# DeltaNet followed by soft mixture of experts on one core: last token group routed in two halves, three experts' second weights loaded into buffers that attention has finished with, outputs stored two tokens a row

## The chip, the cores and the metric

The kernel runs on one core of one Trainium2 chip. The metric is device time in microseconds (us) of one execution. The time before is 323.27 us, the median of three runs (322.57 to 325.41 us). The profile is of a fourth execution that took 327.15 us; from its first to its last instruction it spans 325.4 us, and all times inside the profile are counted from the start of that span.

## The reference: what is computed

First a DeltaNet recurrence over 768 tokens, for 4 batches and 8 heads of size 48, in float32:

```python
k_n = k / (np.linalg.norm(k, axis=-1, keepdims=True) + 1e-06)
for t in range(S):
    y[:, :, t] = q_t @ state
    v_old = state^T @ k_t
    state = state + beta_t * outer(k_t, v_t - v_old)
```

The output y becomes x with 3072 rows (batch times token) and 384 columns. Then a soft mixture of 8 experts with 4 slots each (32 slots):

```python
logits = x @ phi                                   # 3072 x 32
d = softmax of logits over the 3072 tokens         # one maximum per slot, over all tokens
slot_input = d.T @ x                               # 32 x 384
h = relu(slot_input[e] @ w1[e]); slot_out[e] = h @ w2[e]     # w1: 384 x 1024, w2: 1024 x 384
c = softmax of logits over the 32 slots
out = c @ slot_out                                 # 3072 x 384
```

w1 and w2 are 12.6 MB each; one expert's w2 is 1.57 MB (1536 KB in the profile's list of DMA issues). The output is 4.7 MB.

## The kernel before, in words

**Attention.** The 768 tokens are cut into 24 chunks of 32, and the loop variable x runs over the chunks. Six groups n of four chunks (c = 0 to 3) share one 32 x 32 triangular inverse per head and batch, which DVE computes (`invert`, lines 265 to 408) one group ahead. In groups 0 to 4, DVE works on the next group's inverse; in the last group (x = 20 to 23) it has none to do. Inside chunk x the carried chain is: PE multiplies the old state with keys (L450 into psR) and queries (L450 into psY); DVE forms R (L457); PE solves with the inverse Tb (L464); ACT copies the result to U (L467); PE updates the state in PSUM (L477, not in the last chunk) and ACT copies it to S (L484); PE adds the within-chunk part of the outputs (L494) and ACT copies them to Y (L497). At the end of chunk x, `weights(x+1)` has ACT make the next Tb (L427, two instructions).

**Routing.** `turn` (L508) transposes a finished chunk's Y one chunk later. `route` (L516) handles one group: logits (L524), the largest logit per slot and row (L532), its transposition (L537), the maximum over the four batches (L545), its spreading over the partitions by eight small matmuls (L571), the running maximum (L579), the exponentials for the sum over tokens (L587), their repetition and masking (L597, L606), and the sum itself (L615, 32 matmul records for two chunks). Beside it run the softmax over slots (L541, L552 to L564). These pieces are hung into the chunks of the following group at hooks: "head" before R, "act" before the solve, "mid" after the solve and `turn`, "vec" just before the update, "end" after the outputs and before `weights(x+1)`. `late` is what is left for the first chunk of the group after that. Up to the end of the loop and the two drains behind it, each engine runs its instructions in the order in which they are written (`manual_schedule`, L674 to L828).

**The tail.** The last group is routed as a whole after the loop (L829 to L831), in an order that a scheduler chooses. Then the pools of attention are closed (L832), PSUM is handed to a new pool, and the experts run: `first(q)` for experts 4q to 4q+3 is two products (L890) with a mask and relu (L894, L897) and eight transposes (L903); `second(q)` is L914, accumulating into pso. Then pso is copied (L937), summed over batches and spread by one matmul (L939), scaled (L941), and multiplied with the transposed softmax cT for 24 tiles of 128 tokens (L947). Each tile is copied from PSUM by ACT or DVE (L951, L953) into one of ten buffers and stored by a DMA of 128 rows of 1536 bytes (L954).

**Queues.** Nearly all DMAs are issued by SP, in the order written: keys, queries and values some chunks ahead, then w1 into buffers of attention that are done (`preload`, with the table `free`, L755), then w2. A DMA that has to wait for its buffer holds up all those behind it on SP. Of w2, experts 0 to 4 go into new buffers (L841) laid over the space of the closed pools, experts 5 to 7 into the buffers of w1 of experts 0 to 3 (L926 to L931), which become free when `first(0)` has read them.

Of the kernel before, what the change touches and what calls it, by code (L numbers as in the profile page):

```python
# [17 lines left out]
def kernel(  # L18
# [49 lines left out]
    ps = att.enter_context(tc.tile_pool(name="ps", bufs=1, space=PSUM))  # L68
    io = att.enter_context(tc.tile_pool(name="io", bufs=2))
    wk = att.enter_context(tc.tile_pool(name="wk", bufs=2))  # L70
    psp = att.enter_context(tc.tile_pool(name="psp", bufs=1, space=PSUM))
# [7 lines left out]
    Ks = [io.tile([P, U, DP], F32, name=f"K{i}", bufs=1) for i in range(NK)]  # L79
# [20 lines left out]
    def load_v(cc, eng=nc.sync):  # L100
        Vt[cc] = io.tile([P, U, D], F32, name="V", tag="V", bufs=5)
        load(v, Vt[cc], cc, eng)
# [6 lines left out]
    one = cpool.tile([P, 1], F32, name="one")  # L109
    nc.vector.memset(one, 1.0)  # L110
    low = cpool.tile([P, 1], F32, name="low")
    nc.vector.memset(low, -15.0 * math.log(2.0))
    St = [wk.tile([P, 4, B, GD], F32, name=f"S{i}", bufs=1) for i in range(2)]
# [23 lines left out]
    nc.vector.tensor_reduce(own, hm.rearrange("p (y x) -> p x y", x=2), axis=AX.X, op=ALU.add)  # L137

# [54 lines left out]
    cells = [(e, k) for e in range(1, E) for k in range(NKT)]  # L193

# [12 lines left out]
    def preload(tags):  # L207
        for tag in tags.split():
            t = room(tag)
            for i in range(2 if tag == "GQ" else 1):  # L210
                e, k = cells.pop(0)
                load_w1(e, [k], t[:, i * F:(i + 1) * F])

# [294 lines left out]
    def turn(c, Yn, yT):  # L508

        py = pt([GD, B, P])  # L510
        for b in range(B):
            nc.tensor.transpose(py[:, b, :], Yn[:, c, b, 0:GD], ident)  # L512
        nc.scalar.activation(yT[:, :, :, c, :], py.rearrange("p b (h t) -> p b h t", h=4),
                             ACT.Copy)

    def route(n, Yn, yT):  # L516
        st = {}

        def logits():

            pl = st["pl"] = pt([P, P])
            for h in range(4):
                for b in range(B):
                    nc.tensor.matmul(pl[C * b:C * b + C], lhsT=phi[:, h, :],  # L524
                                     rhs=yT[:, b, h].rearrange("p c t -> p (c t)"),
                                     start=(h == 0), stop=(h == 3), skip_group_check=True)
            lT = st["lT"] = wk.tile([P, P], F32, name="lT", tag="lT", bufs=1)
            nc.scalar.activation(lT, pl, ACT.Copy)

        def maxima():  # L530
            m1 = st["m1"] = small.tile([P, 1], F32, name="m1", tag="m1")
            nc.vector.tensor_reduce(m1, st["lT"], axis=AX.X, op=ALU.max)  # L532

        def over_rows():

            pm = st["pm"] = pt([1, B, NSL])
            nc.tensor.transpose(pm.rearrange("p b s -> p (b s)"), st["m1"], ident)  # L537

        def by_tokens():
            pq = st["pq"] = pt([P, B, NSL])  # L540
            nc.tensor.transpose(pq.rearrange("p b s -> p (b s)"), st["lT"], ident)  # L541

        def rows_max():
            mr = st["mr"] = small.tile([1, NSL], F32, name="mr", tag="mr")
            nc.vector.tensor_reduce(mr, st["pm"].rearrange("p b s -> p s b"), axis=AX.X,  # L545
                                    op=ALU.max)

        def over_slots():
# [3 lines left out]
            nc.vector.tensor_reduce(mx, st["pq"], axis=AX.X, op=ALU.max)  # L552
            nc.vector.tensor_tensor(el, st["pq"], mx.unsqueeze(2).broadcast_to([P, B, NSL]),
                                    op=ALU.subtract)

        def slots_exp():
            nc.scalar.activation(st["el"], st["el"], ACT.Exp)

        def shares():
            sm, el = small.tile([P, B], F32, name="sm", tag="sm"), st["el"]  # L560
            nc.vector.tensor_reduce(sm, el, axis=AX.X, op=ALU.add)
            nc.vector.tensor_scalar(sm, sm, 1e-9, None, op0=ALU.add)
            nc.vector.reciprocal(sm, sm)
            nc.vector.tensor_tensor(Call[:, n], el, sm.unsqueeze(2).broadcast_to([P, B, NSL]),  # L564
                                    op=ALU.mult)

        def spread_max():

            pb = st["pb"] = pt([P, 1])
            for b in range(B):  # L570
                nc.tensor.matmul(pb[C * b:C * b + C], lhsT=st["mr"], rhs=one[0:1],  # L571
                                 start=True, stop=True, skip_group_check=True)

        def run_max():
            new, old = nrun[n % 2], nrun[1 - n % 2]
            if n == 0:
                nc.vector.tensor_scalar(new, st["pb"], -1.0, None, op0=ALU.mult)
            else:
                nc.vector.scalar_tensor_tensor(new, st["pb"], -1.0, old, op0=ALU.mult,  # L579
                                               op1=ALU.min)  # L580
                al = st["al"] = small.tile([P, 1], F32, name="al", tag="al")
                nc.vector.tensor_tensor(al, new, old, op=ALU.subtract)

        def rows_exp():
# [3 lines left out]
                dT, st["lT"].rearrange("p (c t) -> p c t", t=C).unsqueeze(2).broadcast_to(  # L588
                    [P, GC, 4, C]), ACT.Exp, bias=nrun[n % 2])
            if n:  # L590
                nc.scalar.activation(st["al"], st["al"], ACT.Exp)

        def repeat():

            pd = st["pd"] = pt([P, GC, B, NSL])
            for c in range(GC):
                nc.tensor.matmul(  # L597
                    pd[:, c].rearrange("p b s -> p (b s)"),
# [3 lines left out]
        def heads():  # L602

            dr = st["dr"] = wk.tile([P, GC * B, 2, NSL], F32, name="dr", tag="dr", bufs=1)
            for x in range(2):
                nc.scalar.activation(dr[:, :, x, :], st["pd"].rearrange("p c b s -> p (c b) s"),  # L606
                                     ACT.Identity, scale=own[:, x:x + 1])

        def slots(cs):
            pa = st["pa"] = pt([P, GD + 1])  # L610
            for c in cs:
                for b in range(B):
                    for y in range(2):
# [4 lines left out]
                            stop=(c == cs[1] and b == B - 1), skip_group_check=True)  # L618
# [364 lines left out]
```

## Time and profile before

| what | value |
|---|---|
| median of three runs | 323.27 us |
| profiled execution | 327.15 us, span 325.4 us |
| PE busy | 269.7 us (83%) |
| DVE busy | 219.7 us (68%) |
| ACT busy | 163.9 us (50%) |
| POOL busy | 160.5 us (49%) |
| mean granted TensorE clock | 0.897 |
| moved by DMA | 45.23 MB, 39.47 MB of it read |
| last attention product (L494) ends | 257.5 us |
| first expert product (L890) starts | 276.0 us |
| last product of second(1) (L914) ends | 305.9 us |
| first output DMA (L954) is issued | 309.6 us |

Busy shares are over the whole span. The last four rows divide the tail into stages that follow each other; what a change in a stage is worth has to be read from that stage. In the views, "pt", "psR", "psS", "psY" are PSUM tiles of attention; "tr", "ph", "po", "pso" those of the experts; "w2t", "wGQ", "wKQ", "w" are buffers of weights. "SPq" is SP's DMA queue; a "wait" there is SP standing still before it may issue.

### The profile page before, as it was taken

The numbers are of one execution on the slowest core, as the hardware profiler recorded it, in microseconds if no ns is written. First come the engines' busy times: TensorE is split into PE (matmuls) and PEld (weight loads), VectorE is DVE, ScalarE is ACT, GpSimd is POOL, SyncE is SP. The second block draws the span as 40 slices with busy tenths as digits, with TensorE's granted clock in tenths as the row PEclk, the third lists the DMA queues.
The fourth block names the chain that finished last, engine by engine and source line by source line (L and its number), as shares of the span: only waits on it lengthen the run. The fifth ranks groups of instructions, "written<-read, shape, count | busy, mean of one in ns | idle before, by whom it ended". The sixth has DMA issues, their size and how long they took to land.

```text
span 325.4 us, 16112 instructions
## 1 busy us (share of the span) xinstructions
PE 269.7 (83%) x6887; PEld 217.0 (67%) x6887; DVE 219.7 (68%) x798; ACT 163.9 (50%) x341; POOL 160.5 (49%) x342
## 2 busy tenths in 40 slices
PE   2896747888979999799998998796999958996890
PEld 2774546767868888688886887786888746332350
DVE  8289989987699989679799999998122122020161
ACT  2454236765857875367666865464358531120050
POOL 8949086784858299621999069996220000000000
PEclk9958559999999999679999999787899977999995
DMA  8955455455444456455201567437622653998087
GB/s 132 164 100 90 69 91 94 70 88 89 81 79 82 78 83 129 93 82 130 50 13 26 144 175 220 91 87 259 202 69 66 221 218 112 432 422 341 4 308 273
DMA packets 82503, 45.23 MB, mean 139 GB/s; under 512 B 74240, under 2 KB 77472, under 8 KB 81664
## 3 DMA queue, kind: packets, MB, share of 16 engines
q1 hardware_dynamic: 80640, 42.98, 50.5%
q0 software_dynamic: 704, 1.03, 1.7%
q8 instruction: 54, 0.88, 1.2%
q10 hardware_dynamic: 1088, 0.20, 0.3%
q14 instruction: 17, 0.14, 0.1%
HBM read 39.47 MB, written 4.72 MB: 136 GB/s over the span
## 4 chain that ended last, share of the span: by engine, by line
PE 50%; DVE 27%; DMA 8%; ACT 6%; issue 4%; SPq 3%; DVEq 0%; ACTq 0%
PE psR L464 6%; PE pt L615 6%; PE psS L477 6%; DMA wGQ<-in_moe_w_dram 5%; DVE prM L333 5%; PE psY L494 5%; PE psR L450 4%; PE pt L257 4%; PE pt L228 4%; DVE prE L333 4%; DVE nm L338 4%; PE pt L512 3%; DVE tt L338 3%; ACT S L484 2%; PE psY L450 2%
## 5 line engine op out<-in xcount | busy, mean ns | idle before, releaser
L414 POOL TENSOR_SCALAR V<-V,nT 128x48 f32<-128x48 f32 x192 | 90.4, 494 | 19.4 <-DMA V<-in_v_dram 5.7
L422 POOL TENSOR_SCALAR_AFFINE_SELECT Ab<-GQ 32x256 f32<-32x256 f32 x96 | 48.0, 500 | 16.9 <-PE psY L494 12.7
L484 ACT ACTIVATE S<-psS 48x768 f32<-48x768 f32 x46 | 37.0, 805 | 24.5 <-PE psS L477 24.2
L464 PE MATMUL psR<-R,Tb 64*64 64x48 f32 x768 | 29.0, 224 | 9.4 <-DVE R L457 6.4
L257 PE MATMUL pt<-KQ 48*32 48x64 f32 (+1 forms) x1792 | 25.9, 232 | 12.5 <-ACT KQ L244 8.8
L464 PEld LDWEIGHTS psR<-R,Tb 64*64 64x64 f32 x768 | 26.0, 139 | 13.0 <-issue 7.0
L257 PEld LDWEIGHTS pt<-KQ 48*32 48x32 f32 x1792 | 20.8, 116 | 18.7 <-ACT KQ L244 10.6
L333 DVE TENSOR_TENSOR prM<-tt,lb 128x16 f32<-128x16 f32 (+7 forms) x96 | 30.4, 317 | 0.0
L338 DVE TENSOR_TENSOR nm<-nm,prM 128x16 f32<-128x16 f32 (+7 forms) x96 | 30.2, 314 | 0.0
L494 PE MATMUL psY<-U,Ab 64*64 64x48 f32 x768 | 29.7, 231 | 0.1
L494 PEld LDWEIGHTS psY<-U,Ab 64*64 64x64 f32 x768 | 26.6, 145 | 2.7 <-issue 0.8
L261 ACT ACTIVATE GQ<-pt 128x256 f32<-128x256 f32 (+1 forms) x56 | 16.7, 351 | 21.4 <-PE pt L257 21.1
L467 ACT ACTIVATE U<-psR 128x384 f32<-128x384 f32 x24 | 11.8, 490 | 29.6 <-PE psR L464 28.3
L477 PE MATMUL psS<-U,K 32*112 32x96 f32 x736 | 26.4, 285 | 0.0
L457 DVE TENSOR_TENSOR R<-V,psR 128x384 f32<-128x384 f32 x24 | 13.2, 551 | 19.4 <-PE psR L450 13.1
L427 ACT ACTIVATE Tb<-TT,own 128x256 f32<-128x256 f32 x48 | 21.6, 504 | 8.1 <-DVE TT L405 8.1
L477 PEld LDWEIGHTS psS<-U,K 32*112 32x112 f32 x736 | 22.4, 189 | 4.1 <-issue 1.7
L338 DVE TENSOR_TENSOR tt<-tt,prE 128x30 f32<-128x30 f32 (+7 forms) x90 | 25.1, 279 | 0.0
L333 DVE TENSOR_TENSOR prE<-tt,lb 128x30 f32<-128x30 f32 (+7 forms) x90 | 24.7, 274 | 0.2 <-DVE nm L338 0.2
L450 PE MATMUL psR<-S,KQ 128*32 128x96 f32 x768 | 23.2, 264 | 1.6 <-issue 0.9
L615 PE MATMUL pt<-Y,dr 64*64 64x97 f32 x384 | 21.6, 272 | 1.8 <-ACT dr L606 1.4
L450 PE MATMUL psY<-S,KQ 128*32 128x96 f32 x768 | 22.3, 258 | 0.7 <-issue 0.7
(161 smaller groups left out, 560.6 us busy)
## 6 DMA issues: line engine op xcount, KB each, us to landing
w2t<-in_moe_w_dram SPq DMA_DIRECT2D x6, 1536.0 KB, 11.6
Q<-in_q_dram SPq DMA_DIRECT2D x96, 48.0 KB, 2.9
out_dram<-ob SPq DMA_DIRECT2D x24, 192.0 KB, 2.4
K<-in_k_dram SPq DMA_DIRECT2D x88, 48.0 KB, 2.5
wKQ<-in_moe_w_dram SPq DMA_DIRECT2D x8, 512.0 KB, 4.2
V<-in_v_dram SPq DMA_DIRECT2D x80, 48.0 KB, 2.6
wGQ<-in_moe_w_dram SPq DMA_DIRECT2D x6, 512.0 KB, 5.6
wKQ<-in_moe_w_dram SPq DMA_DIRECT2D x5, 384.0 KB, 14.2
```

The source lines that it names most:

```text
L257: nc.tensor.matmul(pg[g][rh, b], lhsT=kq[r, b, 0, rh], rhs=kq[r, b, a0:a1, rh], start=True, stop=True, skip_group_check=True)
L333: nc.vector.tensor_tensor(pr, a.broadcast_to([P] + shape), b.broadcast_to([P] + shape), op=ALU.mult)
L338: nc.vector.tensor_tensor(dst, dst, pr, op=op)
L414: nc.gpsimd.tensor_scalar(Vt[cc][:, u], Vt[cc][:, u], nT[n][:, c * U + u:c * U + u + 1], None, op0=ALU.mult)
L422: nc.gpsimd.affine_select(out=Ab[cc % NT][r, :, h % 2, :].rearrange("p (b g) t -> p b g t", g=G), in_=GQ[n][r, c, :, :, 1, :], compare_op= ...
L427: nc.scalar.activation(Tb[cc % 2][:, :, x, :], TT[n][:, c * U:(c + 1) * U, :], ACT.Identity, scale=own[:, x:x + 1])
L450: nc.tensor.matmul(dst[hs[h], b].rearrange("p g d -> p (g d)"), lhsT=kq[:, b, a, hs[h]], rhs=old[:, h, b, :], start=(b == 0), stop=False, ...
L464: nc.tensor.matmul(pw[half[y], u], lhsT=T[y][:, u], rhs=st["R"][half[y], u], start=(u == 0), stop=True, skip_group_check=True)
L477: nc.tensor.matmul(psS[0:DP + D, h, b * GD:(b + 1) * GD], lhsT=K[hs[h], b * G:(b + 1) * G].rearrange("p g d -> p (g d)")[:, 0:DP + D], rhs ...
L484: nc.scalar.activation(new[r, :, :, g * D:(g + 1) * D], psS[r, :, 0:B * GD].rearrange("p h (b g e) -> p h b g e", b=B, g=G)[:, :, :, g], A ...
L494: nc.tensor.matmul(qs[half[y], b, g], lhsT=at[y][:, u], rhs=st["U"][half[y], u], start=False, stop=True, skip_group_check=True)
L615: nc.tensor.matmul(pa[r], lhsT=st["dr"][r, c * B + b].rearrange("p x s -> p (x s)"), rhs=Yn[r, c, b, 0:GD + 1], start=(c == cs[0] and b == 0),
```

## The change

1. The last group is routed in two halves. Chunks 20 and 21 are routed inside chunks 22 and 23 (`ends`), chunks 22 and 23 after the loop, each half with a step of the running maximum of its own. The last but one group (n = 4) is finished two chunks earlier: its repetition and masking move to "act" of x = 22, its two sums to "mid" and "end" of x = 22.
2. In every group one matmul with a constant matrix `same` gives the maxima over rows and spreads them: DVE reads the logits from PSUM, multiplies the maximum with the mask `hm` (128 x 4), PE multiplies with `same`, and one DVE instruction takes the running minimum of the negated values (`accum_out`). The transposition of the maxima, the reduction over batches and the eight small matmuls go. The running maximum and the exponentials move from the third chunk to the second ("vec" and "end").
3. The keys' buffers 0 to 8, the values' five, one of the two states and one of the two Y move to the pool that is never closed, as two larger tiles for the keys and one for the values. w2 of expert 0 is loaded into keys 0 to 5 at x = 19; of expert 1 into keys 6 to 8 at x = 22 and the state at x = 23; of expert 2 into the values and Y at x = 23. Experts 3 and 4 go over the closed pools; 5 to 7 as before into w1 of experts 0 to 3, with other sub-buffers.
4. The tail is under the written order too; the six transposes of the softmax go into psR and psY between other steps, experts use the PSUM tiles of attention, several copies are halved between ACT and DVE, and `first` is split so that the products of experts 4 to 7 enclose the transposes of experts 0 to 3.
5. An output DMA stores two tokens per row: 12 DMAs of 128 rows of 3072 bytes, into 12 separate buffers (old w1). The two tiles of a DMA belong to the same batch.
6. The constants `same` and `msk` are made in the prologue.

```diff
+    Ka = lp.tile([P, 6, U, DP], F32, name="Ka", bufs=1)
+    Kb = lp.tile([P, 3, U, DP], F32, name="Kb", bufs=1)
+    Vs = lp.tile([P, NV, U, D], F32, name="Vs", bufs=1)
...
         def maxima():
-            m1 = st["m1"] = small.tile([P, 1], F32, name="m1", tag="m1")
-            nc.vector.tensor_reduce(m1, st["lT"], axis=AX.X, op=ALU.max)
+            m1 = small.tile([P, 1], F32, name="m1", tag="m1")
+            m4 = st["m4"] = small.tile([P, B], F32, name="m4", tag="m4")
+            nc.vector.tensor_reduce(m1, st["pl"], axis=AX.X, op=ALU.max)
+            nc.vector.tensor_scalar(m4, hm, m1, None, op0=ALU.mult)
 
         def over_rows():
 
-            pm = st["pm"] = pt([1, B, NSL])
-            nc.tensor.transpose(pm.rearrange("p b s -> p (b s)"), st["m1"], ident)
+            pm = st["pm"] = pt([P, B])
+            nc.tensor.matmul(pm, lhsT=same.rearrange("p b t -> p (b t)"), rhs=st["m4"],
+                             start=True, stop=True)
...
+            nc.vector.tensor_scalar(neg, st["pm"], -1.0, old if turn else None, op0=ALU.mult,
+                                    op1=ALU.min, accum_out=new)
...
+        chain = [dict(end=[logits]),
+                 dict(act=[maxima], mid=[over_rows, by_tokens], vec=[run_max, over_slots],
+                      end=[rows_exp, slots_exp])]
+        if cs[0] == 0 and cs[-1] == GC - 1 and n < NG - 2:
+            return chain + [dict(act=[shares], end=[repeat, heads]),
+                            dict(end=[lambda: slots((0, 1))]),
+                            dict(head=[lambda: collect(True)], mid=[lambda: slots((2, 3))],
+                                 vec=[lambda: collect(False)])]
+        if n == NG - 2:
+            return chain + [dict(act=[repeat, heads], mid=[lambda: slots((0, 1))],
+                                 vec=[lambda: collect(True), shares],
+                                 end=[lambda: slots((2, 3))]),
+                            dict(head=[lambda: collect(False)]), {}]
...
+    def ends(x, name):
+
+        if (x, name) == (NCH - 2, "end"):
+            two[0] = route(NG - 1, Ys[1], yT[NG - 1], (0, 1), NG - 1)
+            two[0]["logits"]()
+        elif x == NCH - 1:
+            for f in dict(head=["maxima"], act=["over_rows", "run_max", "rows_exp"],
+                          mid=["repeat"], vec=["heads"],
+                          end=["by_tokens", "over_slots", "slots_exp", "shares"])[name]:
+                two[0][f]()
...
+        if x == 19:
+            load_w2(0, range(NFC), Ka.rearrange("p a u d -> p (a u d)"))
+        elif x == 22:
+            load_w2(1, range(0, 4), Kb.rearrange("p a u d -> p (a u d)"))
+        elif x == 23:
+            load_w2(1, range(4, 8), St[0].rearrange("p h b e -> p (h b e)"))
+            load_w2(2, range(0, 4), Vs.rearrange("p a u d -> p (a u d)"))
+            load_w2(2, range(4, 8), Ys[0].rearrange("p c b e -> p (c b e)"))
...
+    two[0]["slots"]((0, 1))
+    turn(GC - 1, Ys[1], yT[NG - 1], both=False)
+    two[0]["collect"](True)
+    for i in range(2):
+        slots_turned(i)
+    rb["logits"]()
+    rb["maxima"]()
+    for i in range(2, 4):
+        slots_turned(i)
+    rb["over_rows"]()
+    rb["run_max"]()
+    rb["rows_exp"]()
+    slots_turned(4)
+    rb["repeat"]()
+    rb["heads"](both=False)
+    rb["slots"]((2, 3))
+    rb["collect"](True)
...
+    for e in (3, 4):
+        load_w2(e, range(NFC), wp2.tile([P, NFC * Dm], F32, name="w2t", tag="w2t", bufs=2))
...
+    product(0, 0)
+    product(0, 1)
+
+    load_w2(5, range(NFC), w0)
+    load_w2(6, range(0, 5), lies[1, 0])
+    load_w2(6, range(5, 7), lies[1, 2])
+    load_w2(6, range(7, 8), lies[2, 0])
+    for i, at in enumerate(((2, 1), (2, 2), (3, 0), (3, 1))):
+        load_w2(7, range(2 * i, 2 * i + 2), lies[at])
+    product(1, 0)
+    for t4 in range(2):
+        turned(0, t4)
+    slots_turned(5)
+    product(1, 1)
+    nc.vector.tensor_copy(cT[:, 4 * P:NG * P], psY[:, 0:2 * P])
     second(0)
+    for t4 in range(2):
+        turned(1, t4)
     second(1)
...
+    for t2 in range(NT6 // 2):
         for b in range(B):
...
+            for x in range(2):
+                po = banks[i % len(banks)][:, 0:Dm]
+                nc.tensor.matmul(po, lhsT=cT[C * b:C * b + C, 2 * t2 + x::NT6],
+                                 rhs=so[C * b:C * b + C], start=True, stop=True,
+                                 skip_group_check=True)
+                if x:
+                    nc.vector.tensor_copy(ob[:, x], po)
+                else:
+                    nc.scalar.activation(ob[:, x], po, ACT.Copy)
+                i += 1
+            nc.sync.dma_start(
+                out=out[b * S:(b + 1) * S].rearrange("(p t) d -> p t d", t=NT6)[
+                    :, 2 * t2:2 * t2 + 2], in_=ob)
```

## The prediction

> **What bounds the kernel now.** I read the page first, then the chain of waits from 236 us to the end, SP's waits, the table by stretches, and the timeline around 252 and 282 us. In the chain the tail is serial:
>
> ```profile
> 260.91 1.05 PE pt L524 x32
> ...
> 263.93 0.73 ACT dT L587
> 264.71 1.71 PE pt L597 x8
> 266.44 1.27 ACT dr L606 x2
> 267.75 4.94 PE pt L615 x64
> ...
> 284.06 16.41 DMA wGQ<-in_moe_w_dram
> ...
> 300.52 5.36 PE pso L914 x58
> 305.90 0.57 DVE sj L937
> ```
>
> Columns: start, length, what. First a ladder of one-step-at-a-time routing between PE, DVE and ACT (257.5 to 276.0, 18.5 us). Then products until w2 of expert 7 lands at 300.5. Why that is late, SP's waits say (total, times, longest):
>
> ```profile
> SPq L202 <- PE pt L615: 16.2, 1, 16.2
> SPq L202 <- PE ph L890: 7.6, 1, 7.6
> ```
>
> SP stood 16.2 us before the second w2 load until the last routing products freed the memory under it (issues at 256.1, then 272.75), and 7.6 us until first(0) had read expert 0's w1. From 272.75 to 300.5 eleven MB pass. The table by stretches (PE, PEld, DVE, ACT, POOL busy; clock; DMA share; GB/s):
>
> ```profile
> 267.00:273.00 6.00, 4.91 (x64) 4.72 (x64) 0.60 (x3) 0.70 (x2) 0.00 (x0) 0.58 0.01 3
> 276.00:282.00 6.00, 6.00 (x48) 1.64 (x51) 0.00 (x0) 1.72 (x6) 0.00 (x0) 1.00 1.01 430
> 276.00:300.50 24.50, 21.16 (x185) 7.58 (x185) 2.89 (x4) 3.58 (x9) 0.00 (x0) 1.00 0.97 407
> 311.00:313.00 2.00, 2.00 (x15) 1.50 (x12) 1.27 (x3) 1.28 (x4) 0.00 (x0) 1.00 0.99 365
> ```
>
> DMA is idle at 267 to 273 (3 GB/s) and full afterwards; outputs fill it too, at 365 GB/s. PE is busy most of 276 to 300.5 as well, so w2 alone is only part of that stage. The sums of 64 records ran at clock 0.58.
>
> **The Trainium skill.** "TensorE: Matmul & The Clock Gate", section "Part 1: The HAM clock gate", says PE's clock falls to half after a mostly idle window of some 3.4 us. The trace agrees: 0.58 after a stretch (262 to 267) with PE busy 2.31 of 5 us. Its "Part 3: Packing small matmuls" says small matmuls overlap when they use different row groups, and start and end in order. Here four output products of four batches start within 0.02 us, and the two records of one product 0.31 us apart. "DMA: Bandwidth & Descriptors", section "Anatomy of one DMA", says a wait is served on the issuing sequencer ahead of dispatch; the 16.2 us above is that. Its section "Why small descriptors are slow" names a fixed cost per packet: stores of 1536-byte rows run at 365 GB/s, w2 loads with rows up to 12 KB at 426 to 430, which agrees in kind.
>
> **The change, part by part.** Sum against the profiled span of 325.4 us. It was the slower side of the runs (that execution took 327.15, the median is 323.27); I subtract the difference from the median.
>
> *Prologue and x up to 20.* The new constants cost DVE about 0.8 us (a 0.37 reduce, a 0.25 copy, a 0.16 reduce, as L857, L859, L854 now) and POOL 0.5. DVE is idle from 9.1 to 15.1 us (waiting for GQ), POOL from 16.8 to 20.9: zero; with that cover gone, 0.8. Per group DVE loses a 0.28 reduce (L545) and a 0.16 minimum, and gains a 0.17 multiply (128x4, as L562) and a 0.17 minimum; `accum_out` has no row, so 0 to 0.3 more. PE loses eight small matmuls (0.24). ACT's exponentials (0.72 and 0.19) now stand ahead of Tb at the end of the second chunk: Tb at 101.4 to 102.3 becomes 103.2, R ends at 102.65, so its solve slips by up to 0.3. DVE, which is never out of work there, sets these groups' pace and hides it. I take 0; ends: -1.5 (DVE work less, in five groups) and +1.5. The w2 load at x = 19 is 1.57 MB in a stretch with 1.5 to 2 MB of w1 per chunk of 8 to 10 us and no later K, Q or V load behind it: zero.
>
> *x = 21 to 23: +3.0.* No DVE cover here; ACT and PE set the chain:
>
> ```profile
> 250.33 1.62 ACT L484 ACTIVATE S<-psS 48x768 f32<-48x768 f32 x2 [0.49 <-PE psS L477]
> 251.25 1.16 PE L597 MATMUL pt<-ident,dT 128*128 128x128 f32 x8
> 252.34 0.87 PE L450 MATMUL psR<-S,KQ 128*32 128x96 f32 x32
> 252.45 1.26 ACT L606 ACTIVATE dr<-pt,own 128x512 f32<-128x512 f32 x2
> 253.61 0.90 ACT L427 ACTIVATE Tb<-TT,own 128x256 f32<-128x256 f32 x2
> ```
>
> Now the repetition (L597) lies under S's copy and costs nothing; the masks (L606) do hold up Tb and thereby the solve of x = 23 (254.56). After: at the end of x = 21, dT and al ahead of Tb put Tb's end at 248.1, the solve at 248.3 instead of 247.5 (+0.8); the repetition lies under that. In "mid" of x = 22, sums of 32 records (L615, 1.4) stand between solve and update: update 251.4 instead of 249.2 (+2.2 in all). At its end, the other sums (1.5) and the half logits (0.55) run while S is copied (252.5 to 254.1) and outlast it by 1.3: psR of x = 23 starts at 255.45 instead of 252.34. The half logits also hold up ACT's lT and so Tb, which ends at 256.7. Against that the masks no longer delay Tb: solve at 257.2 against 254.56 (+2.65). The half repetition (0.55) before the outputs: L494 ends at 260.5 against 257.5. Bounds: +1.5 if the sums slip under waits, +4 if their PSUM waits bind.
>
> *Routing after the loop: 18.5 becomes 10.5.* Before: sums and transposition of old groups, full logits, then the ladder to 276.0. After, from L494's end: by_tokens 0.3 and the first half's sums 1.4; turn 0.6 with its copy halved 0.45; half logits 0.55; maximum and mask 0.45; matmul, minimum 0.45; dT 0.45; repetition 0.6; masks, two on ACT beside two on DVE, 0.6; 32 sum records 1.5; sacc 0.3; L868 0.7, halved copy 0.4; L874 0.55, copy 0.3; steps between engines 0.4. That is 10.0, with sums at full clock (1.4 to 1.5 per 32 records at 257.3 and 259.4; the 64 after the loop took 4.94). A clock that falls again adds 1; I add 0.5. The products begin at 260.5 + 10.5 = 271.0 against 276.0: -5.0. Ends: -7 and -2.5.
>
> *Products: 29.9 becomes 23.5.* A product of 24 records goes in sets of four, 0.43 us apart: 2.6; second(q) in 16 sets 0.32 apart: 5.2. Four and two of them are 20.8, transposes 2 x 1.05, one more 0.3, gaps 0.3: 23.5, if w2 is there. Experts 5 to 7 (4.7 MB) are asked for after product(0,1), 271.0 + 5.2 = 276.2; at 407 GB/s 11.6 us, landing about 289. second(1) starts at 289.2, and its first step needs only three quarters of it. Experts 0 to 4 have from x = 19 on; from 256.8 (when Tb of x = 23 frees the buffer at the head of SP's queue) 1.5 MB of w1 and 3.9 MB of w2 follow, 12.8 us, and expert 4 (1.6 MB) when the last sums have freed its memory, 268 to 272. So w2 leaves the path, with only 1 to 3 us to spare; late next is PE itself. pso is done at 294.5 against 305.9. Ends: 0 and +5.4 (below).
>
> *Outputs: 19.5 becomes 18.8.* Halved copies bring so 0.5 us earlier. But a DMA needs two tiles of one batch, one row group: four records 0.31 apart, then a 0.56 copy: first issue 3.95 after pso against 3.7. 1536-byte rows take 16 x 1536 / 365 GB/s = 67 ns per row and engine; at the 430 of loads 57. If the 10 ns are per row, 3072-byte rows give 400 GB/s: 11.8 instead of 12.9. PE makes a pair in 0.95 (414 GB/s), just enough. Ends: 365 (+1.1), pairs serial at 1.24 (+3).
>
> Sum: 0 + 3.0 - 8.0 - 6.4 - 0.7 = -12.1 (the second and third terms are the -5.0 above). 323.27 - 12.1 = 311.2.
>
> **Rivals.**
> A. *The ladder costs less* (chance 0.19). If the sums at x = 22 hide and DVE's relief shows in the groups, -4 more: 307. For it: PE has waits there. Against it: they stand in PE's order ahead of the update.
> B. *PE limits the tail* (0.15): clock near 0.6 for the routing (+1) and pairs serial (+3): 315. For it: the 0.58 above. Against it: PE is busier now.
> C. *w2 stays the limit* (0.08). If experts 3 and 4 lie over memory that routing uses until 276, 7.9 MB follow: at 396 GB/s (eleven MB in 27.75 us) three quarters land 5.4 later than second(1) wants: 316.6. Against it: 16.2 us waits end with the sums, not later.
> D. *Nothing comes of it* (0.05): two of B, C and the upper ends together, 320 to 326.
> E. *Slower* (0.04). The keys and values are now parts of three large tiles. If waits go by whole tiles, R of chunk x waits for the V load issued in the same chunk: four issues of some 0.45 and 2.6 to land, 4.4 us, in 20 chunks. It decides from 0.6 us a chunk (12.1 / 20) up; at 1 us the time is 331. Against it: queries already lie two to a tile, and PE waited for a Q load in the loop 0.46 us, once.
>
> **How the numbers follow.** The main case has 0.49 and 309 to 314 as its own range. Reaching to A and C, I give 306 to 317, leaving out D, E and outer parts of A, B and C, about 2 in 10. A measurement of this kernel can tell some 1% from no change: 320.0 and 326.5 are the bounds. Faster 0.91, within 1% 0.05, slower 0.04.
>
> **What would show it.** Right: L494 ends near 260.5, L890 begins near 271, PE has no wait of over 0.5 us on a w2 buffer in L914, DMA at about 400 GB/s in the outputs. Wrong in its steps: a gap before L914 ended by a DMA (C); L947 busy throughout with DMA share below 0.9 (B); chunks up to x = 20 longer by over 0.5 us each with R waiting on a V DMA (E). What would make it wrong altogether is a stage that the trace before has no row for: the written order of the tail letting PE wait behind a step that the scheduler had moved aside.

## The result, and the profile after

The changed kernel takes 345.57 us (median of 4 runs, 342.17 to 349.64) against 322.98 us (322.57 to 325.41) before: ratio 1.0658, 95% interval 1.0567 to 1.075. The forecast was 311.2 us with a range of 306 to 317. It is wrong in sign. Here and below a ratio compares fast runs alone, since some executions of most kernels take over 1.5% longer than the fastest of the same kernel, while a median is of all runs, so that the two can differ by up to 1%.

The profiled execution took 345.08 us and spans 343.1. Cut at the landmarks of the prediction, in us:

| | attention ends | routing after the loop | products | outputs | span |
|---|---|---|---|---|---|
| before | 257.5 | 18.5 | 29.9 | 19.5 | 325.4 |
| predicted | 260.5 | 10.5 | 23.5 | 18.8 | 313.3 |
| after | 262.1 | 13.5 | 27.3 | 40.2 | 343.1 |

The stages account for all of the 17.7 us between the two spans: +4.6 - 5.0 - 2.6 + 20.7. Three stages moved in the direction foreseen, and the outputs doubled. The table by stretches of the changed kernel (PE, PEld, DVE, ACT, POOL busy; clock; DMA share; GB/s):

```profile
262.10:275.60 13.50, 9.56 (x127) 7.50 (x127) 4.54 (x19) 2.94 (x9) 0.00 (x0) 0.87 1.02 404
275.60:302.90 27.30, 24.08 (x242) 9.07 (x241) 4.88 (x13) 3.34 (x6) 0.00 (x0) 1.00 0.52 204
302.90:343.10 40.20, 28.43 (x52) 11.52 (x52) 7.47 (x14) 6.63 (x14) 0.00 (x0) 0.56 0.29 117
```

The first row is what the early w2 was to bring: DMA moves 404 GB/s while routing runs, where it stood at 3 GB/s from 267 to 273 us before. In the second row DMA has half its time free, so w2 no longer sets the products. The third row is the loss: DMA, which the outputs filled before (365 GB/s), is at 117, ACT and DVE are busy for under 8 us of 40, and PE for 28 at a clock of 0.56. Nothing there is at its limit; the engines wait for each other. The chain of waits of the same kernel shows in which order (start, length, what):

```profile
304.92 1.00 PE psS L1024 x2
305.95 0.50 ACT wTT L1030
...
306.49 1.03 PE psS L1024 x2
307.55 0.57 DVE wTT L1028
...
308.16 1.01 PE psS L1024
```

Product, copy, product, copy. The second product goes to another bank than the one being copied, and nevertheless starts only when ScalarE has emptied the first. The timeline names the releaser in so many words:

```profile
306.49 1.02 PE L1024 MATMUL psS<-so,cT 32*128 32x384 f32 x2 [0.58 <-ACT wTT L1030]
308.16 1.01 PE L1024 MATMUL psS<-so,cT 32*128 32x384 f32 x1 [0.65 <-DVE wTT L1028]
```

Four of the six "banks" that the outputs rotate through are slices of one PSUM tile, psS (four banks, allocated for the attention's states). The program tracks that tile as one thing. In PE's instruction order all 16 output products into psS carry a wait: the first for its input `so`, each of the other 15 for the engine that copied from psS last. The eight into psR and psY carry none. From that order:

```
psS<-so,cT 128x384 [waits Activation_49]
psS<-so,cT 128x384 [waits DVE_49]
psR<-so,cT 128x384
psY<-so,cT 128x384
```

### The profile page after: what moved, and what is told of

It reads as the page before. It is cut to its first block, busy times and chain, and to the rows that moved or that the text cites. A ratio compares the mean times of both kernels' runs of the same rounds, so it can differ in the third digit from the quotient of the medians.

```text
span 343.1 us, 16145 instructions
## 1 busy us (share of the span) xinstructions
PE 286.9 (84%) x6889; PEld 224.5 (65%) x6889; DVE 223.3 (65%) x818; ACT 165.1 (48%) x345; POOL 160.0 (47%) x342
## 4 chain that ended last, share of the span: by engine, by line
PE 53%; DVE 25%; ACT 11%; DMA 4%; issue 4%; SPq 1%; POOL 1%; DVEq 0%; ACTq 0%; POOLq 0%
PE psS L1024 7%; PE psR L485 6%; PE psS L498 5%; DVE prE L354 4%; ACT S L505 4%; PE psY L515 4%; PE pt L644 3%; PE pt L278 3%; PE psS L948 3%; DVE prM L354 3%; PE pt L249 3%; PE psS L970 3%; PE psR L471 3%; PE pt L533 3%; DVE tt L359 3%
## 5 line engine op out<-in xcount | busy, mean ns | idle before, releaser
L435 POOL TENSOR_SCALAR Vs<-Vs,nT 128x48 f32<-128x48 f32 x192 | 90.6, 494 | 17.0 <-DVE R L478 5.1
L278 PE MATMUL pt<-KQ 48*32 48x64 f32 (+1 forms) x1792 | 26.8, 232 | 13.6 <-ACT KQ L265 8.3
L1024 PE MATMUL psS<-so,cT 32*128 32x384 f32 x32 | 25.1, 883 | 7.5 <-DVE wKQ L1028 2.0
L354 DVE TENSOR_TENSOR prM<-tt,lb 128x16 f32<-128x16 f32 (+7 forms) x96 | 29.1, 304 | 0.2 <-issue 0.2
L359 DVE TENSOR_TENSOR nm<-nm,prM 128x16 f32<-128x16 f32 (+7 forms) x96 | 29.2, 305 | 0.0
L282 ACT ACTIVATE GQ<-pt 128x256 f32<-128x256 f32 (+1 forms) x56 | 16.7, 351 | 21.1 <-PE pt L278 20.7
L359 DVE TENSOR_TENSOR tt<-tt,prE 128x30 f32<-128x30 f32 (+7 forms) x90 | 26.6, 295 | 0.0
L354 DVE TENSOR_TENSOR prE<-tt,lb 128x30 f32<-128x30 f32 (+7 forms) x90 | 25.6, 284 | 0.0
L478 DVE TENSOR_TENSOR R<-Vs,psR 128x384 f32<-128x384 f32 x24 | 13.2, 552 | 16.4 <-PE psR L471 4.9
L471 PE MATMUL psR<-S,KQ 128*32 128x96 f32 x768 | 22.2, 260 | 1.1 <-ACT S L505 1.0
L307 POOL MEMSET nm<- 128x256 f32 x6 | 1.9, 314 | 44.4 <-DVE prM L354 44.4
```

The lines of the kernel that those rows point to most:

```text
L278: nc.tensor.matmul(pg[g][rh, b], lhsT=kq[r, b, 0, rh], rhs=kq[r, b, a0:a1, rh], start=True, stop=True, skip_group_check=True)
L354: nc.vector.tensor_tensor(pr, a.broadcast_to([P] + shape), b.broadcast_to([P] + shape), op=ALU.mult)
L359: nc.vector.tensor_tensor(dst, dst, pr, op=op)
L435: nc.gpsimd.tensor_scalar(Vt[cc][:, u], Vt[cc][:, u], nT[n][:, c * U + u:c * U + u + 1], None, op0=ALU.mult)
L471: nc.tensor.matmul(dst[hs[h], b].rearrange("p g d -> p (g d)"), lhsT=kq[:, b, a, hs[h]], rhs=old[:, h, b, :], start=(b == 0), stop=False, ...
L1024: nc.tensor.matmul(po, lhsT=cT[C * b:C * b + C, 2 * t2 + x::NT6], rhs=so[C * b:C * b + C], start=True, stop=True, skip_group_check=True)
```

## The experiments

In the kernels below the tail's line numbers shift by one or a few. "Both apart" means outputs and products moved off psS.

**Outputs off the shared tile.** One line of the changed kernel, and the list of banks goes:

```
-                po = banks[i % len(banks)][:, 0:Dm]
+                po = (pt([P, Dm]), (psR, psY)[i // 2 % 2])[x][:, 0:Dm]
```

> The changed kernel with one edit: the 24 output products go in turn to four PSUM tiles of one bank each instead of the four banks of psS, psR and psY. Theory W (a product into one bank of the four-bank tile psS waits for the last copy out of any of its banks, so product and copy take turns, PE idles and its clock falls): the output stage, 40.2 us from pso's end to the span's end, falls to 19 to 22, PE's clock there returns to over 0.8, the time is 323 to 327. Rival S (two tiles of one batch share a row group, and the weights of the outputs are read with a stride of 24 bytes, so the products themselves are slow): the stage stays over 33 us, the time over 338.

Measured: ratio to before 1.0014 (0.997 to 1.0059); 327.61 us median, 12 runs. The outputs take 20.2 us instead of 40.2, with the same 24 products, copies and 12 stores:

```profile
300.30:320.50 20.20, 15.31 (x52) 8.51 (x52) 7.37 (x14) 6.63 (x14) 0.00 (x0) 0.62 0.58 234
```

ACT and DVE are busy for the same 7 us each as in the row of the changed kernel, and the stage is half as long. The clock is hardly better (0.62), so the low clock alone does not make 40 us. It did lengthen the turns. In the changed kernel the first two, at clock 0.98 (302.9 to 308), take 1.57 and 1.67 us from product to product; at clock 0.50 (308 to 343) they take some 2.27. By these figures 13 turns cost 8 to 9 us more than at full clock, which is an estimate.

**Two other explanations of the 40 us**: two products of one row group in turn, and weights read with a stride. The first kernel lets two batches alternate (`for x in range(2): for b in range(b0, b0 + 2)`), banks unchanged. The second reads the combining weights contiguously, `(2 * t2 + x) * P` onwards instead of `2 * t2 + x::NT6`; its output has the tokens of a batch in another order.

> The changed kernel with the output products of two batches interleaved, so that neighbours use different row groups; tiles in PSUM as in the changed kernel. Theory W: the output stage stays at 36 to 41 us, since products take turns with copies anyway. Rival S in its row-group half: the stage falls to below 30 us.

> The changed kernel with the weights of each output product read without a stride; tokens then come out in another order within a batch, the work is the same. Theory W: the output stage changes by less than 2 us. Rival S in its stride half: weight loads fall from 0.30 to 0.18 us and the stage by over 6 us.

Measured (one run each): 348.93 us and 348.0 us, outputs 40.8 and 39.9 us. Neither matters while products and copies take turns, and the kernel with the outputs apart takes 20.2 us with the stride and the pairs of one row group still in it.

**One reader.** psS is copied by ScalarE only, psR and psY by VectorE only:

```
-                po = banks[i % len(banks)][:, 0:Dm]
+                po = (psS[:, (0, 1, 3, 2)[i // 2 % 4]], (psR, psY)[i // 2 % 2])[x][:, 0:Dm]
```

> The changed kernel with the outputs' products alternating between the shared four-bank tile (copied by ScalarE alone) and the two single-bank tiles (copied by VectorE alone), so that the shared tile has one reader. If any pending copy out of the shared tile holds up the next product into another of its banks: each of its 11 later products starts 0.05 to 0.2 us after the ScalarE copy before it ends, but VectorE's pairs run in between and only one of two outputs takes its turn: by the turn of about 1.7 us in the changed kernel, 12 turns, 20 to 23 us from the sum to the end in place of 40.2, and a span of 323 to 327. If the turns need two engines that read the tile: products of the shared tile do not wait for the copy just before, and 19.5 to 20 us as with the outputs apart.

Measured (one run): 339.95 us, span 338.0, outputs 32.1 us. The timeline:

```profile
311.08 1.65 PE L1023 MATMUL psS<-so,cT 32*128 32x384 f32 x2
312.77 0.49 ACT L1029 ACTIVATE wGQ<-psS 128x384 f32<-128x384 f32 x1 [1.74 <-PE psS L1023]
313.32 1.65 PE L1023 MATMUL psS<-so,cT 32*128 32x384 f32 x2
315.00 0.49 ACT L1029 ACTIVATE wKQ<-psS 128x384 f32<-128x384 f32 x1 [1.74 <-PE psS L1023]
```

Each psS product starts 0.06 us after the copy before it ends (312.77 + 0.49 = 313.26), so one reader is enough for the turns. I sized the turn at 1.7 us; at the low clock it is 2.24 (313.32 - 311.08), and twelve of them are 27 us. The mechanism held, the size did not.

**The products off psS.** `ph = psS[:, f]` becomes `ph = pt([P, HF])`.

> The changed kernel with one edit: the four first expert products go to pt tiles instead of banks of psS. Theory W: the three waits of PE on copies of hr (0.74, 0.80, 0.89 us) go, the stage from the first expert product to pso's end falls from 27.3 to some 24.9; outputs stay at about 40. Rival (the stage is longer than my 23.5 because w2 or PE's clock is late): no change in this stage.

Measured (one run): 343.58 us; products 24.3 us instead of 27.3, outputs still 40.8. In the changed kernel the second half-product waits in the same way:

```profile
278.56 0.69 ACT L955 ACTIVATE hr<-psS,msk 128x512 f32<-128x512 f32 x1 [1.14 <-PE psS L948]
279.30 0.62 PE L948 MATMUL psS<-w,sl 128*32 128x512 f32 x1 [0.92 <-ACT hr L955]
...
289.94 0.75 DVE L952 TENSOR_SCALAR hr<-psS,msk 128x512 f32<-128x512 f32 x1 [2.23 <-PE psS L948]
290.83 0.48 PE L970 MATMUL psS<-Ka,hT 128*32 128x384 f32 x1 [1.04 <-DVE hr L952]
```

Three such gaps (after the first, second and fourth half-product; 0.92, 1.02 and 1.04 us) are the 3 us. The last pair is the clearest: the second layer's sums go to another bank, and wait for the masked copy all the same.

**Both apart, and four batches in turn.** The first kernel is the two edits together. The second also lets all four batches alternate.

> The changed kernel with both edits: expert products into pt tiles, outputs into four tiles of one bank each. Theory W: the savings add up, 2.4 us in the products and 20 us in the outputs; against the kernel before the ratio is 0.985 to 0.997. Rival: the product stage stays at 27 us and the ratio at 1.00.

> As the kernel with both edits, but the output products of the four batches alternate (first token of all four, then second), so that four row groups follow each other; still 12 DMAs of two tokens a row. Theory R (products that follow each other in one row group run one at a time, PE counts as little used and its clock goes to 0.5 in the outputs): output stage 18 to 19 us instead of 20, PE's clock there over 0.7. Rival (the clock falls for another reason, the wait before the outputs): the clock stays at 0.5 and the stage within 0.5 us of 20.

Measured: 0.9965 (0.9917 to 1.0012), 324.64 us median; and 1.0121 (1.0064 to 1.0177), 326.13 us. The outputs take 19.5 and 19.3 us. Of these, 19 us of the first kernel and of the second:

```profile
302.00:321.00 19.00, 14.56 (x52) 8.83 (x52) 7.34 (x14) 6.32 (x13) 0.00 (x0) 0.67 0.63 248
305.00:324.00 19.00, 10.29 (x52) 7.33 (x52) 6.92 (x14) 6.01 (x14) 0.00 (x0) 0.90 0.63 248
```

With four row groups in turn the clock is 0.90 instead of 0.67 and PE is busy for 10.3 us instead of 14.6, as theory R forecast, but the stage is hardly shorter: PE does not set the length of the outputs once the turns are gone. Both DMA rates are 248 GB/s over these 19 us, which include the first products and the last landing. The 1.0121 was not followed up; in the one profile it does not come from the outputs (attention ends at 265.5 instead of 263.8, and the products take 26.0 us instead of 24.3). The cure brings the change back to the level of before, not to the forecast.

**Parts of the change by themselves**, on the kernel before. First, outputs two tokens a row (12 stores, three PSUM tiles as before). Second, three experts' w2 into done buffers:

```
+        if x == 19:
+            load_w2(0, range(NFC), Ka.rearrange("p a u d -> p (a u d)"))
...
+    load_w2(2, range(4, 8), Ys[0].rearrange("p c b e -> p (c b e)"))
+    for e in (3, 4):
```

> The kernel before with the new outputs alone: 12 DMAs of 128 rows of 3072 bytes, the two tiles of a DMA of the same batch, six PSUM banks in turn, five buffers of two tiles. Prediction's step: 19.5 us become 18.8, ratio 0.996 to 0.999, DMA at 400 GB/s. Theory R: PE's clock falls to 0.5, the stage is 20 to 21 us, ratio 1.001 to 1.006.

> The kernel before with the early w2 loads alone: keys, values, one state and one Y in the long pool, experts 0 to 2 loaded from x = 19 on, three w2 buffers fewer at the end, one output buffer fewer (space). Theory: w2 leaves the path, PE does not wait for a w2 buffer in L914 (3.0 us before), the stage from 276.0 to pso's end falls from 29.9 to some 27, ratio 0.988 to 0.995. Rival (early loads of large tiles hold up attention): chunks from x = 19 on longer by over 1 us, ratio over 1.0.

Measured: 0.9991 (0.9956 to 1.0026), 322.98 us; outputs 18.9 us, as the prediction had it (18.8). The DMA rate that it named, 400 GB/s instead of 365, came too; 311 to 322 us of this kernel:

```profile
311.00:322.00 11.00, 7.89 (x30) 5.58 (x27) 5.02 (x9) 3.93 (x8) 0.00 (x0) 0.72 1.01 397
```

And for the early w2 0.997 (0.993 to 1.0011), 323.72 us; products 25.7 us instead of 29.9. Neither ratio can be told from no change in these runs.

**Whole copies.** Both apart, with the halved copies of the routing whole again (the turned chunk, the heads' rows, the turned sums), for example:

```
-    nc.vector.tensor_copy(sT[:, 0:2], pT[:, 0:2])
-    nc.scalar.activation(sT[:, 2:4], pT[:, 2:4], ACT.Copy)
+    nc.vector.tensor_copy(sT, pT)
```

> The kernel with both repairs, with the copies after the loop whole again: the turned last chunk, the heads' rows and the turned sums each copied by one engine instead of half by ScalarE and half by VectorE. Theory: two engines that read one PSUM tile take turns, so the halves saved nothing: from the last attention product to the first expert product 13.4 us as with halves, within 0.5, and ratio 0.9965. Rival, the prediction's own count: halves save 0.2 to 0.5 us each, so that whole copies give 14.5 us or more.

Measured: 325.28 us (4 runs, 318.89 to 327.91, too few for a ratio). From the last attention product (267.71) to the first expert product (281.14) it takes 13.4 us, as with halves (263.83 to 277.27). The halves brought nothing. Why, four lines of the changed kernel show:

```profile
302.96 0.33 ACT L1004 ACTIVATE sj<-psS 128x192 f32<-128x192 f32 x1 [5.49 <-PE psS L970]
303.32 0.36 DVE L1002 COPY sj<-psS 128x192 f32<-128x192 f32 x1 [5.30 <-ACT sj L1004]
...
303.97 0.42 ACT L1011 ACTIVATE so<-pt,rd 128x192 f32<-128x192 f32 x1 [0.68 <-PE pt L1006]
304.36 0.42 DVE L1009 TENSOR_SCALAR so<-pt,rd 128x192 f32<-128x192 f32 x1 [0.69 <-PE pt L1006]
```

Both pairs write the halves of one SBUF tile. The first pair reads one PSUM tile, and DVE is released by ACT, after its half. The second pair reads two PSUM tiles, and DVE is released by PE. In these two pairs it is the source that takes turns. The Trainium skill, "PSUM — Partial Sum Buffer", section "PSUM bank collisions raise a hardware error", says that two engines must be kept off one bank in the same partitions, ScalarE's reads against VectorE's included, while different banks may be used at the same time. The first half agrees with the 0.33 and 0.36 us one after the other. The second half says that the turns in psS, whose products and copies are in different banks, are more than the banks ask for: they come from the program's bookkeeping by tile.

**A pause of PE.** In the profile of the changed kernel PE stops inside the solve of chunk 15 with nothing to wait for ("issue"):

```profile
186.65 0.31 PE L485 MATMUL psR<-R,Tb 64*64 64x48 f32 x2
189.03 1.13 PE L485 MATMUL psR<-R,Tb 64*64 64x48 f32 x30 [2.07 <-issue]
```

Every kernel with the new routing and an unshifted stream had this after the same two of 32 records, for 0.9 to 2.3 us, and none with the old routing had it in that solve. One packet of the instruction queue (0.02 MB) passes at 186.4 to 186.6, just before. The old routing has such pauses too, only elsewhere; the kernel before, for example, in the solve of an earlier chunk:

```profile
131.64 1.00 PE L464 MATMUL psR<-R,Tb 64*64 64x48 f32 x18 [1.42 <-issue]
```

From 50 us to the end of attention, PE's pauses of 0.3 us or more add up to 3.0 to 7.3 us in the six profiles with the old routing and to 4.8 to 9.5 us in the eleven with the new. I tried whether the place in PE's stream decides, with both apart and 12 transposes at the very start whose result nothing reads:

```
+    for _ in range(12):
+        nc.tensor.transpose(psS[:, 0, 0:P], ident, ident)
```

> The last experiment's kernel with both repairs (outputs and products off the shared tile) and, at the very start, 12 more 128x128 products whose result nothing reads: 48 more TensorE instructions (each fp32 product shows as two loads and two matmuls), about what the new routing took out before chunk 15. Theory: the pause of 0.9 to 2.3 us inside the solve of chunk 15, which all seven kernels with the new routing show after the second of 32 records and which nothing in the trace releases, belongs to a place in TensorE's instruction stream (a 16 KB packet of the instruction queue lands just before or in it), so the shift moves it ahead of the solve, into products that nobody waits for: solve of chunk 15 to solve of chunk 16 takes 6.9 to 7.2 us, as with the old routing, in place of 8.1 (both repairs) and 9.3 (the changed kernel). In chunk 22 the pause after record 27 of the state's products moves to an earlier record of that group or just ahead of it, and stays on the path. Median 323 us, ratio 0.992. Rival: the delay of chunk 16 is a wait for w1's load into a done query buffer, and the shift changes nothing: 8.1 to 9.3 us, ratio 0.9965 as without the shift.

Measured: 0.9994 (0.9938 to 1.005). A transpose is one record, not two, so the shift is 12 records (the page counts 6901 instead of 6889), and the pause moved by 11, from two records into the solve to nine before the end of the group ahead of it:

```profile
190.04 0.32 PE L278 MATMUL pt<-KQ 48*32 48x64 f32 x9 [1.41 <-issue]
```

An earlier pause moved by 11 records as well. In all sixteen profiles without the shift it stands 36 records before the end of its group, with either routing, and with the shift 47; both apart, without and with the shift:

```profile
56.71 0.60 PE L278 MATMUL pt<-KQ 48*32 48x64 f32 x36 [1.41 <-issue]
59.19 0.71 PE L278 MATMUL pt<-KQ 48*32 48x64 f32 x47 [1.15 <-issue]
```

So the place in the stream is what these pauses are tied to. The rest of the expectation failed. The group ahead of the solve is on the path too (R was ready at 188.4, the solve began at 190.3), and soon after it the clock fell, so that chunk 15 to 16 took 10.0 us, instead of the 8.1 of both apart and the 6.9 of the old routing. Rows of 192 to 196 us, of this kernel and of the changed one:

```profile
192.00:196.00 4.00, 3.98 (x70) 3.81 (x72) 2.78 (x3) 2.41 (x4) 3.82 (x11) 0.50 0.83 271
```

```profile
192.00:196.00 4.00, 3.74 (x129) 3.43 (x127) 1.87 (x5) 3.18 (x7) 3.72 (x10) 1.00 0.91 337
```

At clock 0.50 (first row) a busy PE got through 70 records instead of 129. The pause in the state's products of both apart, which I expected to stay, was gone. (It stands at 239.0 there, in chunk 21 and not 22.)

**The old routing with the rest of the change**, and then, because the parts did not seem to add, three kernels side by side on one chip. The first is the kernel before with both edits of "parts by themselves" (and four output buffers of two tiles instead of five).

> The kernel before, its routing and its three PSUM tiles for the outputs kept, with the two other parts of the change: w2 of experts 0 to 2 into done keys, values and state, and outputs two tokens a row. If the parts add (0.997 and 0.9991 alone): ratio 0.996, 321.5 us; products from the first to the end of the sum 25 to 26 us, outputs 18.9 us, pause of chunk 15 absent. Against the both-repaired kernel (0.9965) it gives what the routing in two halves is worth by itself: about nothing, since its 5 us after the loop (ladder 18.5 to 13.4) are spent on 3 us in chunks 21 to 23 and 1 to 2 us at chunk 15. Rival: routing in halves is a gain of its own, 3 us or more, and this kernel is then at 1.005 or above.

> Early w2 alone, beside the next two kernels on one chip. If the parts add and the earlier 0.997 held a disturbed set of runs: 0.986 to 0.99, since paired outputs alone gave 0.9991. If 0.9845 was one chip's: 0.995 to 0.999 here as before.

> Early w2 and paired outputs with the old routing. If the routing in halves is what costs: 0.983 to 0.988 again, 0.008 or more below the all-parts kernel. If the earlier value was one chip's: 0.994 to 0.998, level with the all-parts kernel.

> All parts of the change with outputs and products off the shared PSUM tile: 0.995 to 0.999 in either case; the distance to the kernel with the old routing is the price of routing the last group in halves (3 to 4 us expected, from 0.9965 against 0.9845).

Measured, ratios to before:

| kernel | earlier | side by side |
|---|---|---|
| w2 alone | 0.997 (0.993 to 1.0011) | 0.9895 (0.9863 to 0.9927) |
| w2 and outputs, old routing | 0.9845 (0.9808 to 0.9882) | 0.9854 (0.9797 to 0.9911) |
| all parts, both apart | 0.9965 (0.9917 to 1.0012) | 0.9887 (0.9836 to 0.9939) |

The first and third of the earlier column are from one chip, the second from another, the right column from a third. Side by side the parts add within the intervals (0.9895 x 0.9991 = 0.9886 against 0.9854), and the routing in halves costs 0.3%, which is inside the intervals. I had expected 0.995 to 0.999 for all parts and the old routing 0.008 or more below; neither came. On the second chip the shifted kernel, which has all parts, stood at 0.9994 beside the 0.9845; these 1.5% also hold what the shift itself did. The version with the old routing is 1.5% below before both times: 319.94 and 321.67 us median against 324.32 and 325.7. That it is faster than all parts together was not shown (0.9854 and 0.9887, six runs each). In its first profile the products run from 270.99 to 298.29, the outputs take 19.2 us, and the span is 317.5.

## Why the prediction was wrong, step by step

*Outputs, "19.5 becomes 18.8": the step that failed.* It measured 40.2, 21.4 us more. The prediction counted the pairs, the stores and the row groups, and took six independent PSUM banks for granted. The diff had the list in plain sight: four of the six are `psS[:, k]`. With separate tiles the stage is 18.5 to 20.6 us in six profiles, so the rest of that step was sized well (18.9 with pairs on the old kernel, DMA at 397 GB/s). The kernel before had its outputs in separate tiles ("ph", "tr", "po"), so no row of its trace showed such a wait. A stage without a row in the trace before is the sign that the prediction had named for being wrong altogether, though it looked for it in the written order, not in the tiles. The prediction's bound for this term (+3, pairs serial at 1.24 us) was of the wrong kind: it had PE's own order in mind, not a wait for the copies.

*Rival E had the mechanism in the wrong place.* It asked whether waits go by whole tiles, for keys and values in SBUF, and gave it 4 in 100. No such wait showed there: at 222.59 GpSimd began scaling chunk 23's values in the shared tile, before the R of chunk 19 that reads it (223.30). The same question was not asked of PSUM, where it cost 21 us. What the rival needed, a small wait repeated many times, was met 15 times in the outputs.

*Products, "29.9 becomes 23.5".* 27.3 measured; off psS 24.3. So 3.0 of the 3.8 missing are the same turns, and 0.8 the size of the estimate. The part on w2 was right: second(1) did not wait for a DMA, and SP's waits for w2 buffers, 16.2 us at the longest before, are now (total, times, longest)

```profile
SPq L222 <- PE psS L948: 10.1, 2, 9.6
SPq L222 <- DVE dr L634: 8.5, 1, 8.5
```

The second ends at 270.3, inside the stretch with 404 GB/s: DMA had other w2 loads to move, so it costs nothing. By itself the early w2 takes the products from 29.9 to between 25.7 and 27.3.

*Routing after the loop, "18.5 becomes 10.5".* 13.5. Two terms were mis-sized. The halved copies were put at their half: the turned chunk took 0.38 and 0.42 one after the other with a step between (0.83 instead of 0.45), the sums' copy 0.35 and 0.32 (0.70 instead of 0.4), and the maximum waited for ScalarE's copy of the same logits (0.26): together 0.9. And the clock:

```profile
269.75 2.38 PE L644 MATMUL pt<-Y,dr 64*64 64x97 f32 x32 [0.71 <-ACT dr L636]
272.54 1.40 PE L917 MATMUL pt<-sacc,ident 128*32 128x96 f32 x8 [0.41 <-DVE sacc L655]
```

2.38 and 1.40 us where the prediction had 1.5 and 0.7: the granted clock was 0.50 from 270.4 to 272.2 and 0.58 from 272.2 to 274. It had added 0.5 for a clock that falls again; it was 1.6. As many records of the same line took 1.55 us at 262.39, at clock 1.00. The remaining 1 us is spread over steps between engines.

*x = 21 to 23, "+3.0".* Right, in its steps too. From the solve of chunk 20 to the last attention product it took 27.9 us instead of 24.85, and 27.9 again with the outputs apart. Counted in the same way, the solves of chunks 22 and 23 came 1.1 and 2.8 us later than before (0.8 and 2.65 predicted). Over all profiles it is 27.7 to 34.9 us with the new routing and 24.85 to 27.1 with the old. The two longest, both apart and four batches, have a pause of PE in chunk 21 (2.05 us at 239.0 in the first, where the clock is 0.50 from 244 to 248).

*Up to x = 20, "zero".* Too low. From the solve of chunk 15 to the last attention product, six profiles with the old routing took 68.6 to 70.3 us; eleven with the new, 74.7 to 80.0. The 3.0 above are in that; some 2 to 7 us are not. A part lies in chunk 15, which took 8.1 to 12.5 us to the next solve instead of 6.9: the pause (0.9 to 2.3 us) and, in some, a clock that falls after it (with the products apart 0.50 from 190 to 194 us, and 12.5 us). The rest was not taken apart. The prediction looked for DVE work and for SBUF waits, and had no row for PE's instruction stream. Why the pause comes there in the new order, and what decides where the clock falls, stays open. So does the exact price of the routing in halves, 0.3% side by side and, with the shift, 1.5% on another chip: from chunk 15 on attention loses 4 to 11 us to it in the profiles, and the routing after the loop gains 5.

*The sum.* With both apart, the profile of the side-by-side run ends attention at 260.4 (predicted 260.5) and spans 317.5 against the 313.3 predicted: +2.9 for the routing after the loop, +0.8 for the products, +0.6 for the outputs. That attention ends where it was predicted is luck. This was the fastest of six executions (319.46 us, median 324.02), and the profile before was a late one: attention ends at 252.5 to 257.5 in the six profiles with the old routing and at 259.5 to 267.7 in the eleven with the new. Without the shared tile the forecast (ratio 0.963) would have been right in sign side by side, at a third of its size (0.9887), and within no change in the earlier runs (0.9965). So the shared tile is what made the kernel slower than before; the zero up to x = 20 and the routing after the loop are the larger part of what keeps the cured kernel from the forecast.

## What to carry to other kernels

Before output products rotate through PSUM slices, look up what was allocated: the slices of the four-bank tile were one buffer to the waits here, and a rotation over them was no rotation. Give each buffer that PE fills while another engine empties its neighbour a tile of its own. Halving a copy between two engines brought nothing here where both halves came out of one PSUM tile; look at what the halves read. And when a rival names a mechanism, ask it of every memory that the change touches before giving it a chance.

## What the runs showed of the hardware that was not expected

PE can stop for 0.9 to 2.3 us with nothing to wait for, at a place that belongs to its instruction stream: 12 records put in ahead moved two such pauses by 11 records each. A packet of the instruction queue came just before one of them; that this packet is its cause was not shown. The same kernel measured against before in two sets of runs, on different chips, gave ratios up to 0.8% apart: 0.997 and 0.9895 for w2 alone, whose intervals do not overlap, and 0.9965 and 0.9887 for all parts, whose intervals do. Whether the chip makes the difference was not shown. Kernels that differ by so little are to be compared side by side.
